# Second layer of a mixture of experts on one core: three token blocks by seven half-width products each, with sums carried between PSUM banks

## The chip, the core and the metric

The kernel runs on one core of a Trainium2 chip. TensorE (PE) multiplies 128x128 tiles; VectorE (DVE), ScalarE (ACT) and GpSimd (POOL) do everything else; DMAs are issued from SyncE (SP). The time is that of the device for one execution, in microseconds (us): the median of three executions unless it is called the profiled one. The changed kernel is timed on the same inputs.

## The reference

Gated linear attention over 4 batches, 8 heads, 768 steps and 48 channels gives x, a 3072 x 384 matrix; router weights P come from its logits by eight Sinkhorn rounds; eight experts then act on every token, each with a hidden layer of 1024.

```python
state = f[:, :, t, :, None] * state + np.einsum('bhd,bhe->bhde', k[:, :, t], v[:, :, t])
y[:, :, t] = np.einsum('bhd,bhde->bhe', q[:, :, t], state)
...
P = np.exp(logits)
for _ in range(8):
    P /= P.sum(1, keepdims=True) + 1e-09
    P /= P.sum(0, keepdims=True) + 1e-09
    P *= N / E
...
for e in range(E):
    h = np.maximum(x @ w1[e], 0.0)
    ye = h @ w2[e]
    out += P[:, e:e + 1] * ye
```

Everything is in float32. The kernel splits each factor of a product into a high and a low fp16 part and sums three matmuls (high with high, low with high, high with low), so one product costs three.

## The kernel before

**Two phases.** Up to about 491 us the attention is computed in chunks, with the plain products of experts 0 and 1 between them; their outputs go unscaled to DRAM, since P isn't known yet, and are fetched, scaled and added later ("re-adds": `yb` by DMA, `yz` by ScalarE, the sum by GpSimd). Phase 2 has 48 periods, for experts 2 to 7, both halves m of the hidden layer and the four batches (`ORDER`). A batch is 768 tokens; a period covers 512 hidden rows of one expert on one batch.

**A period.** The first layer is done by a fast matrix scheme: 15 products on sums of blocks of w1 (`k1`) and of x (`xah`, `xbh`), one per slot (`SLOTS`), each of six matmuls of 256 columns. They accumulate in six PSUM banks named A to F; between them `EVENTS` names what happens after a slot: a copy of a bank to SBUF (ScalarE, `cp`), an add of a copy to a bank (DVE), an init of a fresh bank from another bank and a copy (DVE), and the conversion of a finished bank into the fp16 left factors of the second layer: `kh`/`kl` for a plain half, `kah`/`kal`, and by way of float32 sums `kr`, `kf` the pairs `kgh`/`kgl`. A bank must be complete before the next product adds to it: the init of F reads D, so the third product into D (slot 13) waits for it.

**Second layer before.** Of the three 256-token blocks of a period, t = 0 and 1 are `paired`: the 2 x 2 block product is done with seven half-width products instead of eight (`product`, 42 matmuls of 192 columns), whose partial sums are copied out by ScalarE (`part`), added by GpSimd (L1254, L1255) and DVE (L1257, L1260, L1263) and evicted by DVE (L1216) or by ScalarE and GpSimd (L1219, L1220). Block t = 2 is `plain`: 24 matmuls of 384 columns, evicted by ScalarE and GpSimd. A budget (`drain`) spreads these matmuls over the slots of the next period, from slot `LAG` = 2.

**Weights.** `prepare_w1` and `prepare_w2` run beside it as lists of steps, each at a given slot after its period n (`at_all`, `plan`): a DMA, sums by GpSimd (`k1s`, `k2s`), a maximum over the raw tile for a later check (`wmx`, DVE), high parts by ScalarE and low parts by DVE (`k1l`, L1039; `k2l`, L1053; `k2sl`, L1081). A w1 tile and a w2 tile are prepared in every second period, over some 25 to 39 slots; so an even and an odd period differ, and a pair of them is the unit that repeats.

The order of instructions on every engine is the order in which the program issues them (`pin`, `mm`), whichever is ready. PSUM has eight banks: six rotate for the first layer (`pk`, tag k), two hold second-layer sums (`psm`).

## Time and profile before

| | |
|---|---|
| median of three executions | 1511.97 us (1510.23 to 1512.18) |
| the profiled execution | 1511.74 us, span of its instructions 1510.0 us |
| granted TensorE clock, mean | 0.996 |
| phase 1 | 0 to about 491 us |
| phase 2, 48 periods | about 491 to 1502 us, 20.65 us a period in its steady part |

A row of a timeline has the start, the length, the engine, the line, the operation, what it writes and reads, its shape, and, in brackets, how long the engine had been idle and what ended that. Groups give the total and the mean in ns; a mean includes the latency of one operation, so neighbours overlap by a little. In windows, each engine's busy time stands behind the length of the stretch. A line of waits has the waiting engine and operation, what it waited for, the total, the count and the longest.

### The profile page before, as it was taken

Reading aid. Unit: us, or ns where it says so; the run is one execution under the profiler, and the core shown is the slowest. Engines: PE = TensorE matmul, PEld = TensorE weight load, DVE = VectorE, ACT = ScalarE, POOL = GpSimd, SP = SyncE. Lnnn points to the kernel's source line nnn. Section 1 sums busy time; section 2 is a strip of 40 time slices with the busy share of each in tenths; the row PEclk is TensorE's granted clock in tenths of the full one; section 3 lists DMA queues with packets and bytes.
Section 4 is the critical chain, followed back from the end, with each engine's and each line's share of the span. In section 5 each row is a group of like instructions: output and inputs, shape, how many; then the busy total and the mean of one; then the engine's idle time right before and its main releaser. Section 6 shows DMA issues by size and latency. Waiting matters only on the chain.

```text
span 1510.0 us, 37891 instructions
## 1 busy us (share of the span) xinstructions
PE 1477.1 (98%) x15185; PEld 1213.1 (80%) x15185; DVE 1282.7 (85%) x2352; ACT 1002.8 (66%) x2103; POOL 968.4 (64%) x1154
## 2 busy tenths in 40 slices
...
DMA packets 82794, 95.85 MB, mean 63 GB/s; under 512 B 49872, under 2 KB 66384, under 8 KB 82608
## 3 DMA queue, kind: packets, MB, share of 16 engines
...
## 4 chain that ended last, share of the span: by engine, by line
PE 88%; DVE 7%; ACT 2%; issue 1%; POOL 1%; DMA 1%; DVEq 0%; POOLq 0%; ACTq 0%
PE kyps L287 21%; PE yps L287 13%; PE kxps L287 12%; PE hps L287 10%; PE kb_A L287 8%; PE kb_B L287 8%; PE kb_D L287 6%; PE kb_C L287 4%; PE kb_E L287 2%; PE kb_F L287 2%; PE kvps L287 1%; PE aps L287 1%; DMA w1r<-in_w_dram 1%; DVE kf L1375 1%; POOL k1s L1026 0%
## 5 line engine op out<-in xcount | busy, mean ns | idle before, releaser
L287 PEld LDWEIGHTS <-k1h 128*128 128x128 f16 x2880 | 282.1, 98 | 38.7 <-DVE kl L1392 0.5
L1220 POOL TENSOR_TENSOR acc<-acc,yt 128x384 f32<-128x384 f32 x175 | 203.2, 1168 | 105.7 <-ACT yt L1219 101.2
L1387 POOL TENSOR_TENSOR kgl<-kf,kgh 128x512 f16<-128x512 f32 x188 | 217.1, 1165 | 40.9 <-ACT kgh L1384 40.2
L1219 ACT ACTIVATE yt<-kyps,pes 128x384 f32<-128x384 f32 x175 | 103.7, 592 | 131.8 <-PE kyps L287 69.6
L287 PEld LDWEIGHTS <-kh 128*128 128x128 f16 x1536 | 147.3, 98 | 34.8 <-DVE acc L1212 1.5
L287 PEld LDWEIGHTS <-k1l 128*128 128x128 f16 x1440 | 141.1, 98 | 24.6 <-issue 3.6
L287 PEld LDWEIGHTS <-kgh 128*128 128x128 f16 x1536 | 144.3, 98 | 5.3 <-ACT kgh L1384 1.1
L287 PE MATMUL yps<-w2h,hl 128*128 128x384 f16 x384 | 125.5, 327 | 2.8 <-DVE hl L440 2.6
L287 PE MATMUL yps<-w2l,hh 128*128 128x384 f16 x384 | 125.4, 326 | 1.9 <-DVE w2l L359 1.9
L287 PE MATMUL kyps<-k2h,kh 128*128 128x384 f16 x384 | 125.2, 326 | 1.5 <-DVE acc L1212 1.2
L287 PE MATMUL yps<-w2h,hh 128*128 128x384 f16 x384 | 125.5, 327 | 0.2 <-ACT hh L437 0.2
L287 PE MATMUL kyps<-k2h,kl 128*128 128x384 f16 x384 | 125.2, 326 | 0.4 <-DVE kl L1392 0.4
L287 PE MATMUL kyps<-k2l,kh 128*128 128x384 f16 x384 | 125.2, 326 | 0.0
L287 PEld LDWEIGHTS <-w1h 128*128 128x128 f16 x1344 | 97.2, 98 | 34.0 <-issue 3.1
L1384 ACT ACTIVATE kgh<-kf 128x512 f16<-128x512 f32 x192 | 120.7, 629 | 3.6 <-DVE kf L1375 3.5
L1254 POOL TENSOR_TENSOR part<-part 128x192 f32<-128x192 f32 x96 | 57.3, 596 | 88.7 <-DVE kf L1375 61.1
L287 PEld LDWEIGHTS <-hh 128*128 128x128 f16 x768 | 74.6, 98 | 47.7 <-issue 2.5
L1353 ACT ACTIVATE cp<-kb_A 128x512 f32<-128x512 f32 x144 | 87.4, 607 | 21.9 <-PE kb_A L287 21.6
L287 PE MATMUL kyps<-k2sl,kgh 128*128 128x192 f16 x384 | 94.5, 246 | 0.0
L287 PE MATMUL kyps<-k2sh,kgl 128*128 128x192 f16 x384 | 94.5, 246 | 0.0
L287 PE MATMUL kyps<-k2sh,kgh 128*128 128x192 f16 x384 | 94.5, 246 | 0.0
L287 PEld LDWEIGHTS <-kl 128*128 128x128 f16 x768 | 75.1, 98 | 23.3 <-issue 5.3
...
## 6 DMA issues: line engine op xcount, KB each, us to landing
...
```

The lines of the kernel that those rows point to most:

```text
L287: ins = (nc.tensor.transpose if transpose else nc.tensor.matmul)(**kw)
L1219: pin(nc.scalar.activation(out=yt, in_=ps, func=AF.Copy, scale=p))
L1220: pin(nc.gpsimd.tensor_tensor(out=y, in0=y, in1=yt, op=ALU.add))
L1254: pin(nc.gpsimd.tensor_tensor(out=part[:, 1, :], in0=part[:, 1, :], in1=part[:, 2, :], op=ALU.add))
L1353: pin(nc.scalar.activation(out=fresh(ev[2]), in_=bk, func=AF.Copy))
L1375: pin(nc.vector.scalar_tensor_tensor(out=f[:, n], in0=bk[:, :, 128 * v:128 * v + 128], scalar=0.0, in1=other, op0=ALU.max, op1=op))
L1384: pin(nc.scalar.activation(out=hs['g', t][0][:, lo:hi], in_=hs['f', t][:, lo:hi], func=AF.Copy))
L1387: pin((nc.vector if tag == str(PERIODS - 1) else nc.gpsimd).tensor_tensor(out=hs['g', t][1][:, lo:hi], in0=hs['f', t][:, lo:hi], in1=hs['g ...
```

## The change

All three blocks are `paired`, in another form. A block has one bank, `q`, whose first half is x0, and half of another, `p`, with y0 and x1 (the names are the program's: x0, y0 and x1 are 192 wide each). ScalarE moves sums from bank to bank (`move`, L1179 in the changed kernel: y0 to x0, y0 to x1, x1 to `part`, scaled), and PE goes on accumulating there. DVE adds the finished sums, scaled by P, into the output or into an `yraw` tile (L1182), four 192-wide adds for a block (for block 1 ScalarE does two of them as scaled moves), and GpSimd adds the `yraw` tiles to the output (L1218). Each block takes five slots in a fixed pattern: of its 42 matmuls and its neighbours', slots 8 to 12 of a period have 6, 6, 6, 12 and 12, and so on in fives; the blocks of a period start 6 slots into the next one (`LAG`). In PSUM the first layer has five banks (B and D its own, A, F, E and C rotate over k0 to k2), the second layer one for x and two of `psm`.

The w2 tile keeps three of its four quadrants and four sums, in one tile of 7 x 192 columns, high and low. The steps for a w2 tile are eight for nine: the maximum (step two) moves from slot 12 to slot 22 after the period's start, the lows of the quadrants and the sums to slots 29 and 38. The left factors of the third block add conversions: `gd` and `gb` (differences of two tiles, on GpSimd, for block 2 on DVE), `gs` now in three operations, `kgh`/`kgl` in two pieces for each of three blocks. Copies rotate over two buffers for three, the fetched early output `yb` has one buffer for two, and re-adds begin at period 5 for 3. At the end, 23 slots without first-layer work finish the last blocks.

The diff, cut to what is spoken of:

```diff
-          9: (('ga', 'A', 0),), 10: (('copy', 'C', 7), ('gs', 'A', 0, 0), ('gb', 'A', 0)), 11: (('add', 'D', '-', 7),),
-          12: (('init', 'F', '+', 1, 'D'), ('hh', 'B', 1, 0)), 13: (('gs', 'B', 0, 1), ('gs', 'B', 0, 2), ('gs', 'B', 0, 3)),
-          14: (('gh', 0, 0, 2), ('gl', 0, 0, 2), ('sum', 'D', '-', 4, 3), ('hl', 'B', 1, 0)), 15: (('add', 'C', '+', 3), ('hh', 'D', 1, 2), ('gh', 0, 2, 4), ('gl', 0, 2, 4)),
-          16: (('hh', 'C', 1, 1), ('hh', 'F', 0, 2), ('hl', 'D', 1, 2), ('ga', 'E', 1)), 17: (('hs', 'E', 1), ('hl', 'F', 0, 2)),
-          18: (('gs', 'E', 1, 0), ('gb', 'E', 1)), 19: (('gs', 'C', 1, 1), ('gs', 'C', 1, 2), ('gs', 'C', 1, 3)),
-          20: (('gh', 1, 0, 2), ('gl', 1, 0, 2), ('hl', 'C', 1, 1)), 21: (('gh', 1, 2, 4), ('gl', 1, 2, 4))}
-END = 22
-ENDING = (('add', 'gh', 'gl'), ('ga', 'hs', 'hh'), ('gs',), ('gb', 'hl'), ('gh', 'gl', 'late'))
+          9: (('ga', 'A', 0), ('gd', 0, 'P')), 10: (('copy', 'C', 7), ('gf', 'A', 0)), 11: (('add', 'D', '-', 7), ('hs', 'E', 1)),
+          12: (('init', 'F', '+', 1, 'D'), ('hh', 'B', 0), ('ga', 'E', 1)), 13: (('gs', 'B', 0, 1), ('gs', 'B', 0, 2), ('gs', 'B', 0, 3), ('gb', 1, 'P'), ('gd', 1, 'P')),
+          14: (('gh', 0, 0), ('gl', 0, 0), ('sum', 'D', '-', 4, 3), ('hl', 'B', 0)), 15: (('add', 'C', '+', 3), ('hh', 'D', 2), ('gh', 0, 1), ('gl', 0, 1)),
+          16: (('hs', 'F', 2), ('hh', 'C', 1), ('hl', 'D', 2)), 17: (('ga', 'F', 2), ('gd', 2, 'V'), ('gs', 'D', 2, 1), ('gs', 'D', 2, 2), ('gs', 'D', 2, 3)),
+          18: (('gs', 'C', 1, 1), ('gs', 'C', 1, 2), ('gs', 'C', 1, 3), ('hl', 'C', 1), ('gf', 'F', 2)), 19: (('gh', 1, 0), ('gl', 1, 0)),
+          20: (('gh', 1, 1), ('gl', 1, 1)), 22: (('gh', 2, 0), ('gl', 2, 0)), 23: (('gh', 2, 1), ('gl', 2, 1))}
+END = 24
...
-PLAIN, PAIRED = (2,), (0, 1)
+PAIRED = (0, 1, 2)
+BY_POOL = (1,)
+RIGHTS = ((0, 0), (1, 0), (1, 1))
 DH = DM // 2
-PAIR_COST = 0.51
-PAUSE = 5.0
-LAG = 2
+LAG = 6
 STEPS = 8
+FIRST_READD = 5
...
-    def prepare_w2(e, j, plain_first=False):
+    def prepare_w2(e, j):
...
+        wh, wl = (lp.tile([128, 7, DH], F16, name=f"k2{n}_{e}_{j}", tag=f"k2{n}", bufs=4) for n in "hl")
         (b11, b12), (b21, b22) = ((raw[:, f, 0:DH], raw[:, f, DH:DM]) for f in range(2))
+        pieces = ((wh[:, 0, :], wl[:, 0, :], b11), (wh[:, 1:3, :], wl[:, 1:3, :], raw[:, 1, :].rearrange("p (r d) -> p r d", d=DH)))
+        for h_, _, src in pieces:
+            pin(nc.scalar.activation(out=h_, in_=src, func=AF.Copy, scale=W2S))
+        yield
...
+        lows(pieces)
+        yield
+        pin(nc.scalar.activation(out=wh[:, 3:7, :], in_=sums, func=AF.Copy, scale=W2S))
+        yield
+        lows(((wh[:, 3:7, :], wl[:, 3:7, :], sums),))
+        k2[e, j] = wh, wl
...
-    pk = ctx.enter_context(tc.tile_pool(name="pk", bufs=6, space=PSUM, reuse_waits="tile"))
+    pk = ctx.enter_context(tc.tile_pool(name="pk", bufs=1, space=PSUM, reuse_waits="tile"))
...
+    def paired(n, h, t):
         e, m, b = ORDER[n]
-        if n == first[b]:
+        new = n == first[b]
+        if new and t == PAIRED[0]:
             acc[b] = accp.tile([128, 2, TT, DM], F32, name=f"acc{b}", tag="acc")
-
-        def scale(v, t):
+        p = psm.tile([128, DM], F32, name=f"kyps_{n}_{t}", tag="m")
+        q = pk.tile([128, DM], F32, name=f"kxps_{n}_{t}", tag="x")
+        x0, y0, x1 = q[:, 0:DH], p[:, 0:DH], p[:, DH:DM]
+        p2 = lp.tile([128, DH], F32, name=f"part_{n}_{t}", tag="part", bufs=2)
+        by_pool = t in BY_POOL and n < len(ORDER) - 1 and not new
+        xx, yy = (acc[b][:, v, t, :].rearrange("p (s d) -> p s d", s=2) for v in range(2))
+        if not new:
+            yy = rp.tile([128, 2, DH], F32, name=f"yy_{n}_{t}", tag="yraw", bufs=3)
+        if by_pool:
+            xx = rp.tile([128, 2, DH], F32, name=f"xx_{n}_{t}", tag="yraw", bufs=3)
...
+        def move(out, in_, **kw):
+            pin(nc.scalar.activation(out=out, in_=in_, func=AF.Copy, **kw))
+
+        def add(y, ps, p, z):
+            pin(nc.vector.scalar_tensor_tensor(out=y, in0=ps, scalar=p, in1=z, op0=ALU.mult, op1=ALU.add))
...
+        product(y0, None, (0, 0), start=True)
+        product(x1, (None, 0), (None, 0))
+        yield
+        move(x0, y0)
+        move(p2, x1, scale=scale(1))
+        yield
+        product(y0, (None, 2), (None, 2))
+        yield
+        move(x1, y0)
+        yield
+        product(x0, (1, 0), (1, 0), stop=True)
+        yield
+        yield
+        product(x1, (None, 1), (None, 1))
+        yield
+        out_x(0, x0)
+        add(yy[:, 1, :], x1, scale(1), p2)
+        yield
+        product(y0, (1, 1), (None, 3), stop=True)
+        product(x1, (None, 3), (1, 1), stop=True)
+        yield
+        add(yy[:, 0, :], y0, scale(1), p2)
+        out_x(1, x1)
+        for v, z, there in ((0, xx, not by_pool), (1, yy, new)):
+            if not there:
+                y = acc[b][:, v, t, :]
+                pin((nc.vector if n == len(ORDER) - 1 else nc.gpsimd).tensor_tensor(out=y, in0=y, in1=z.rearrange("p s d -> p (s d)"), op=ALU.add))
...
-            at_all(n, (0, 7, 8, 9, 10, 8, 11, 12, 13, 22, 23, 24) if n else (14, 17, 18, 19, 20, 24, 25, 26, 27, 28, 29, 37), gen)
+            at_all(n, (0, 3, 4, 5, 6, 8, 9, 10, 11, 22, 23, 24) if n else (14, 17, 18, 19, 20, 24, 25, 26, 27, 28, 29, 37), gen)
...
-            at_all(n, (10, 12, 18, 22, 23, 26, 26, 27, 38) if n != 3 else (0, 2, 8, 12, 13, 16, 16, 17, 20), prepare_w2(e2, 2 * m2 + part // 2))
-        if 3 <= n:
-            for s in (9, 12):
-                plan.setdefault((n, s), []).append(lambda: readd(False))
+            at_all(n, (10, 22, 25, 26, 27, 29, 35, 38) if n != 3 else (0, 2, 8, 12, 13, 16, 17, 20), prepare_w2(e2, 2 * m2 + part // 2))
+        if n >= FIRST_READD:
+            at_slots(n, (9, 12), again)
...
+    def kbank(n, bk):
+        k = "AFEC".find(bk)
+        tag = bk if k < 0 else f"k{(max(k - 1, 0) + int(n)) % 3}"
+        return pk.tile([128, 2, 256], F32, name=f"kb_{n}_{bk}", tag=tag)
...
+        elif kind == 'gd':
+            r = hs['r', ev[1]]
+            pin((nc.gpsimd if ev[2] == 'P' else nc.vector).tensor_tensor(out=r[:, 0], in0=r[:, 1], in1=r[:, 0], op=ALU.subtract))
...
+    def advance(n, s):
+        k, j = divmod(n * PRODUCTS + s - LAG, 5)
+        k -= TT
+        if k >= 0 and not j and k < PERIODS * TT:
+            going.append(paired(k // TT, helped[k // TT], PAIRED[k % TT]))
+        if not going or j == 1 and len(going) == 1 and k < PERIODS * TT:
+            return lambda: None
+        block = going[0 if j == 1 else -1]
+        next(block)
+
+        def rest():
+            if next(block, going) is going:
+                going.remove(block)
+
+        return rest
```

Two places on DVE where the order of its instructions moves, both in an odd period (period 11, expert 3; k1l and k2l are the low parts of a w1 and a w2 tile, kb_ the first-layer banks, kxps and kyps second-layer sums, yy and acc output sums). The first is from the second layer's sums at slot 7 to the init of F. Before:

```order
L1216 SCALAR_TENSOR_TENSOR acc_9256<-kxps_0_12046,pes,acc_9256 128x384 [waits DVE_49]
L1263 TENSOR_TENSOR kyps_0_12047<-kyps_0_12047,both_0_12049 128x384 [waits PE_49,Pool_49]
L1355 TENSOR_TENSOR kb_B<-kb_B,cp_0_12141 128x512 [waits Activation_49]
L1039 SCALAR_TENSOR_TENSOR k1l_3_11888<-k1s_3_11802,k1h_3_11887 128x640 x2
L1039 SCALAR_TENSOR_TENSOR k1l_3_11888<-k1r_3_11644,k1h_3_11887 128x256
L1039 SCALAR_TENSOR_TENSOR k1l_3_11888<-k1r_3_11644,k1h_3_11887 128x384
L1375 SCALAR_TENSOR_TENSOR kf_0_12177<-kb_A,kr_0_12180 128x256 [waits PE_49,Activation_49,Pool_49]
L1381 SCALAR_TENSOR_TENSOR kal_0_12197<-kb_A,kah_0_12196 128x256
L1355 TENSOR_TENSOR kb_D<-kb_D,cp_7_12221 128x512 [waits PE_49,Activation_49]
L1053 SCALAR_TENSOR_TENSOR k2l_3_12071<-k2r_3_11873,k2h_3_12070 128x384
L1358 TENSOR_TENSOR kb_F<-kb_D,cp_1_12094 128x512 [waits DVE_49]
```

After:

```order
L1182 SCALAR_TENSOR_TENSOR yy_2_12287<-kyps_2_12284,pes,part_2_12286 128x192 [waits PE_49]
L1182 SCALAR_TENSOR_TENSOR acc_8993<-kyps_2_12284,pes,acc_8993 128x192
L1039 SCALAR_TENSOR_TENSOR k1l_3_12115<-k1s_3_11970,k1h_3_12114 128x640
L1047 TENSOR_REDUCE wmx<-k2r_3_12141 128x1 [waits DMAHW1_49]
L1039 SCALAR_TENSOR_TENSOR k1l_3_12115<-k1s_3_11970,k1h_3_12114 128x640
L1039 SCALAR_TENSOR_TENSOR k1l_3_12115<-k1r_3_11883,k1h_3_12114 128x256
L1039 SCALAR_TENSOR_TENSOR k1l_3_12115<-k1r_3_11883,k1h_3_12114 128x384
L1332 SCALAR_TENSOR_TENSOR kal_0_12483<-kb_A,kah_0_12482 128x256 [waits Activation_49]
L1182 SCALAR_TENSOR_TENSOR acc_9363<-kxps_0_12409,pes,acc_9363 128x192 [waits PE_49]
L1182 SCALAR_TENSOR_TENSOR yy_0_12411<-kyps_0_12408,pes,part_0_12410 128x192 [waits PE_49,Pool_49]
L1302 TENSOR_TENSOR kb_D<-kb_D,cp_7_12505 128x512 [waits Activation_49]
L1305 TENSOR_TENSOR kb_F<-kb_D,cp_1_12367 128x512 [waits DVE_49]
```

The reduction wmx now stands between the k1l operations; the adds of the next block (the two behind kal) come ahead of the add to D; the kf operation and the k2l between D and F have gone from here to behind F.

The second place follows it, from the sum of D and the copy cp_4 to the add that completes A, on which the sixth slot of the next period builds. Before:

```order
L1364 TENSOR_TENSOR cp_3_12308<-kb_D,cp_4_12018 128x512 [waits PE_49]
L1392 SCALAR_TENSOR_TENSOR kl_1_0_11980<-kb_B,kh_1_0_11979 128x512
L1257 TENSOR_TENSOR both_1_12251<-kyps_1_12249,part_1_12250 128x192 [waits Activation_49]
L1355 TENSOR_TENSOR kb_C<-kb_C,cp_3_12308 128x512 [waits DVE_49]
L1392 SCALAR_TENSOR_TENSOR kl_1_2_11984<-kb_D,kh_1_2_11983 128x512 [waits Activation_49]
L1260 TENSOR_TENSOR kxps_1_12248<-kxps_1_12248,both_1_12251 128x192 [waits DVE_49,PE_49]
L1216 SCALAR_TENSOR_TENSOR acc_9256<-kxps_1_12248,pes,acc_9256 128x384 [waits DVE_49]
L1263 TENSOR_TENSOR kyps_1_12249<-kyps_1_12249,both_1_12251 128x384 [waits PE_49,Pool_49]
L1392 SCALAR_TENSOR_TENSOR kl_0_2_11978<-kb_F,kh_0_2_11977 128x512 [waits Activation_49]
L1355 TENSOR_TENSOR kb_A<-kb_A,cp_13_12382 128x512 [waits PE_49,Activation_49]
```

After:

```order
L1064 SCALAR_TENSOR_TENSOR k2l_3_12517<-k2r_3_12141,k2h_3_12516 128x192
L1064 SCALAR_TENSOR_TENSOR k2l_3_12517<-k2r_3_12141,k2h_3_12516 128x384
L1302 TENSOR_TENSOR kb_C<-kb_C,cp_3_12616 128x512 [waits DVE_49]
L1182 SCALAR_TENSOR_TENSOR yy_1_12532<-kyps_1_12529,pes,part_1_12531 128x192 [waits PE_49,Activation_49,Pool_49]
L1351 SCALAR_TENSOR_TENSOR kl_2_12250<-kb_D,kh_2_12249 128x512 [waits Activation_49]
L1326 TENSOR_TENSOR kr_2_12679<-kr_2_12679 128x256 [waits Activation_49]
L1323 SCALAR_TENSOR_TENSOR kr_2_12679<-kb_D,kr_2_12679 128x256 [waits DVE_49]
L1323 SCALAR_TENSOR_TENSOR kf_2_12711<-kb_D,kr_2_12679 128x256
L1323 SCALAR_TENSOR_TENSOR kf_2_12711<-kb_D,kf_2_12711 128x256 [waits DVE_49]
L1182 SCALAR_TENSOR_TENSOR yy_1_12532<-kyps_1_12529,pes,part_1_12531 128x192 [waits PE_49]
L1302 TENSOR_TENSOR kb_A<-kb_A,cp_13_12693 128x512 [waits Activation_49]
```

The two k2l stand here now, with the difference, the sums and a low part for block 2 (kr_2, kf_2, kl_2) and two adds of block 1, where the sums of the paired block and its eviction stood.

273 lines of the change are left out of this document (83 added, 190 removed).

## Prediction, made before the changed kernel had run

> **What bounds the kernel now.** I read the page's engine shares first, then its chain that ended last, then the waits of PE, the windows of one pair of periods, and the timeline of four engines inside that pair. The first two, from the page:
>
> ```profile
> PE 1477.1 (98%) x15185; PEld 1213.1 (80%) x15185; DVE 1282.7 (85%) x2352; ACT 1002.8 (66%) x2103; POOL 968.4 (64%) x1154
> PE 88%; DVE 7%; ACT 2%; issue 1%; POOL 1%; DMA 1%; DVEq 0%; POOLq 0%; ACTq 0%
> ```
>
> PE is busy for 98% of the span and carries 88% of the chain. The shares average two phases, so I look at the steady part of phase 2, where the change lies: two periods (an even and an odd one), by windows, and all of PE's waits between 600 and 1400 us.
>
> ```profile
> 868.50:889.20 20.70, 20.70 (x201) 18.13 (x199) 17.45 (x35) 16.40 (x36) 17.57 (x25) 1.00 0.20 59
> 889.20:909.80 20.60, 20.60 (x200) 18.03 (x199) 20.13 (x37) 15.51 (x33) 16.92 (x19) 1.00 0.19 59
> PE kxps L287 <- DVE acc L1216: 0.5, 1, 0.5
> ```
>
> Columns: length, then PE, PEld, DVE, ACT and POOL busy, then the granted clock. PE has no gap, at clock 1.00; the odd period has DVE at 20.13 of 20.60. So the steady part runs as fast as PE issues matmuls, and DVE is right behind it. That is the whole question: PE gets less to do, DVE does not.
>
> **What PE saves.** Matmuls overlap, so their price is the distance of starts, from PE's timeline:
>
> ```profile
> 900.27 0.33 PE L287 MATMUL kyps<-k2l,kh 128*128 128x384 f16 x1
> ...
> 900.75 0.33 PE L287 MATMUL kyps<-k2l,kh 128*128 128x384 f16 x1
> 900.92 0.25 PE L287 MATMUL kxps<-k2h,kah 128*128 128x192 f16 x1
> ...
> 902.56 0.27 PE L287 MATMUL kb_D<-xah,k1h 128*128 128x256 f16 x1
> ...
> 903.22 0.25 PE L287 MATMUL kyps<-k2sh,kgh 128*128 128x192 f16 x1
> ...
> 904.04 0.27 PE L287 MATMUL kb_F<-xah,k1h 128*128 128x256 f16 x1
> ```
>
> Four 384-wide ones from 900.27 to 900.92 are 0.1625 us each, six 256-wide ones from 902.56 to 903.22 are 0.109, ten 192-wide ones from 903.22 to 904.04 are 0.082. A period has 90 first-layer matmuls, 24 wide and 84 narrow second-layer ones: 9.8 + 3.9 + 6.9 = 20.6 us, which is the window's length. After, the 24 wide ones are gone and 42 narrow ones stand for them: 3.90 - 3.44 = 0.455 us less in each of 48 periods, **-21.9 us**.
>
> Narrower matmuls load weights more often. The loads, by line:
>
> ```profile
> L287 PEld LDWEIGHTS <-k1h 128*128 128x128 f16 x2880 | 282.1, 98 | 38.7 <-DVE kl L1392 0.5
> ```
>
> A load's span is 98 ns, over the 82 ns of a narrow matmul, yet ten narrow ones in a row kept 0.082, so spans of loads overlap and I price them at nothing. The Trainium skill ("TensorE: Matmul & The Clock Gate", section "LDWEIGHTS (loading the stationary operand)") puts a load at its columns over 1.2 in ns, so 107 ns for 128; if that paced PE, 42 narrow matmuls would cost an estimated 4.5 us for the 3.9 of the wide ones, and the change would lose 28 us. The 0.082 us spacing above speaks against that as a pace.
>
> **What DVE, ScalarE and GpSimd get.** ScalarE gives up four evictions and copies of a period and gets about six moves of 192; such a copy is two in 0.55 us here, a move between PSUM banks (512 wide) is 0.58:
>
> ```profile
> 902.76 0.55 ACT L1245 ACTIVATE part<-kxps 128x192 f32<-128x192 f32 x2
> 895.21 0.58 ACT L1361 ACTIVATE kb_C<-kb_B 128x512 f32<-128x512 f32 x1
> ```
>
> With the third block's conversions it goes from some 15.6 to 16.1 us of a period of 20.2: room, price nothing. GpSimd, by groups of the page:
>
> ```profile
> L1220 POOL TENSOR_TENSOR acc<-acc,yt 128x384 f32<-128x384 f32 x175 | 203.2, 1168 | 105.7 <-ACT yt L1219 101.2
> L1387 POOL TENSOR_TENSOR kgl<-kf,kgh 128x512 f16<-128x512 f32 x188 | 217.1, 1165 | 40.9 <-ACT kgh L1384 40.2
> L1254 POOL TENSOR_TENSOR part<-part 128x192 f32<-128x192 f32 x96 | 57.3, 596 | 88.7 <-DVE kf L1375 61.1
> ```
>
> It loses four part adds a period (2.4 us), keeps about four output adds, gets two more kgl (2.3 us) and three 256-wide operations (gd, gd, gb: 0.6 each, worked from the 596 ns of a 192): about +2 us, so 18.5 to 19 us of 20.2 while early outputs are re-added. Its queue then runs late by at most some two slots by my count, and the earliest use of a kgl is about four slots off; no price in the sum, a rival below.
>
> DVE's total falls a little (18.7 to about 18.3 us): eight sums and evictions of two blocks, half of them 384 wide, go and ten 192-wide adds come in. But its order changes, and this is where I find the price. The first place in the section on the change shows what DVE has in odd periods between the x1 product of slot 7 and the init of bank F. F must be made before PE may write D again in slot 13 (the init reads D). Two things are new: the reduction wmx of a w2 tile stands between the four k1l operations (its step moved from slot 12 of the even period to slot 7 of the odd one), and four 192-wide adds stand in the stretch where wider sums came and went earlier. Before, the same stretch, DVE and GpSimd:
>
> ```profile
> 894.49 0.69 DVE L1355 TENSOR_TENSOR kb_B<-kb_B,cp 128x512 f32<-128x512 f32 x1
> 895.09 2.35 DVE L1039 SCALAR_TENSOR_TENSOR k1l<-k1s,k1h 128x640 f16<-128x640 f32 x2
> 897.36 1.68 DVE L1039 SCALAR_TENSOR_TENSOR k1l<-k1r,k1h 128x256 f16<-128x256 f32 x2
> 898.96 0.41 DVE L1375 SCALAR_TENSOR_TENSOR kf<-kb_A,kr 128x256 f32<-128x256 f32 x1
> 899.29 0.41 DVE L1381 SCALAR_TENSOR_TENSOR kal<-kb_A,kah 128x256 f16<-128x256 f32 x1
> 899.62 0.68 DVE L1355 TENSOR_TENSOR kb_D<-kb_D,cp 128x512 f32<-128x512 f32 x1
> 900.22 1.30 DVE L1053 SCALAR_TENSOR_TENSOR k2l<-k2r,k2h 128x384 f16<-128x384 f32 x1
> 901.45 0.69 DVE L1358 TENSOR_TENSOR kb_F<-kb_D,cp 128x512 f32<-128x512 f32 x1
> ```
>
> ```profile
> 895.27 1.48 POOL L1220 TENSOR_TENSOR acc<-acc,yt 128x384 f32<-128x384 f32 x1 [0.17 <-ACT yt L1219]
> 896.72 1.90 POOL L1071 TENSOR_TENSOR k2s<-k2r 128x192 f32<-128x192 f32 x2
> 898.58 1.57 POOL L1074 TENSOR_TENSOR k2s<-k2r,k2s 128x192 f32<-128x192 f32 x2
> 900.11 1.00 POOL L1291 TENSOR_TENSOR acc<-acc,yz 128x384 f32<-128x384 f32 x1
> ```
>
> F ended at 902.14 and PE began D at 902.56: a spare of 0.4 us. The four k1l took 3.87 us (895.09 to 898.96) beside a busy GpSimd. Beside an idle one (idle until 565.39, with 2.78 us of wait before), by the timeline:
>
> ```profile
> 562.60 0.81 DVE L1039 SCALAR_TENSOR_TENSOR k1l<-k1s,k1h 128x640 f16<-128x640 f32 x1
> 563.33 0.95 DVE L1081 SCALAR_TENSOR_TENSOR k2sl<-k2s,k2sh 128x768 f16<-128x768 f32 x1
> 564.20 0.82 DVE L1039 SCALAR_TENSOR_TENSOR k1l<-k1s,k1h 128x640 f16<-128x640 f32 x1
> 564.93 0.89 DVE L1039 SCALAR_TENSOR_TENSOR k1l<-k1r,k1h 128x256 f16<-128x256 f32 x2
> 565.39 1.29 POOL L1291 TENSOR_TENSOR acc<-acc,yz 128x384 f32<-128x384 f32 x1 [2.78 <-ACT yz L1290]
> ```
>
> each 640-wide one is 0.73 from start to start and the last two 0.89: 2.35 in all. The k2l at 900.22 ended at 901.52, half a microsecond after GpSimd's add ended at 901.11, as if it had stood until then. The Trainium skill ("SBUF — State Buffer", section "Who interferes with whom") has VectorE and GpSimd arbitrate for one pair of ports with an exclusive lock; the trace agrees, 3.87 us against 2.35.
>
> Now the chain after, from T, PE's start of slot 8. PE reaches D in slot 13 after 3 slots with 6 narrow matmuls (0.655 + 0.492 = 1.15) and 2 with 12 (1.64): T + 6.7. DVE may start the adds when slot 7's last matmul has landed, T + 0.2. It then does one 192-wide add, wmx, the four k1l, kal, two 192-wide adds, D and F. Prices of the two not yet shown, by groups:
>
> ```profile
> L1260 DVE TENSOR_TENSOR kxps<-kxps,both 128x192 f32<-128x192 f32 x77 | 27.4, 356 | 0.0
> L1049 DVE TENSOR_REDUCE wmx<-k2r 128x1 f32<-128x768 f32 x19 | 17.9, 942 | 0.0
> ```
>
> Neighbours start some 0.08 before the end of one (0.81 against 0.73 above), so 0.3 for an add and 0.86 for wmx; kal 0.33 (899.29 to 899.62 above), D 0.68 since F needs its result, F 0.69. Without contention: 0.2 + 0.3 + 0.86 + 2.35 + 0.33 + 0.6 + 0.68 + 0.69 = 6.0, and PE would not wait. With the four k1l at 3.87: 7.5, and PE waits **0.8 to 0.9**. After, GpSimd is fuller than before in this stretch (kgl and output adds at 1.17), so I take the contended price; its own bound above, where each k1l meets a fresh kgl, is another microsecond. Behind F, DVE has the lows of the w2 tile, the gd, gs, gs, gs of block 2 and the adds before it can finish bank A, on which PE's slot 5 of the next period depends: 7.6 us at lone prices, some 9 contended, with a ScalarE copy (0.6) behind, against 9.0 us of PE. I put 0.45 on it (0 to 1). Even periods have about 1.3 us more room and wait for nothing. Together 1.3 us (0.2 to 2.4) in each of the 20 pairs whose w2 tile is prepared in that place: **+26**.
>
> Head and tail, by windows and waits:
>
> ```profile
> 491.90:507.00 15.10, 13.09 (x109) 10.34 (x107) 11.57 (x20) 10.17 (x20) 5.42 (x7) 1.00 0.12 40
> PE kxps L287 <- ACT part L1245: 1.1, 1, 1.1
> PE kxps L287 <- ACT kgh L1384: 0.9, 1, 0.9
> ```
>
> The first 17 slots, with first-layer work alone, took 15.1 us for 11.1 of matmuls; after, the lag is four slots longer, at 0.23 us lost each: +1. The tail's two waits are on conversions and copies, and there will be a third block's: +1.5 (-1 to +3). The first w2 maximum, which now stands in DVE's row in phase 1, I put inside these.
>
> Sum, from the profiled execution's 1511.74 (span 1510.0, and 0.2 below the median): 1511.7 - 21.9 + 26 + 2.5 = **1518.7 us**.
>
> **Rivals.** *PE stays back to back.* If GpSimd's operations fall beside PSUM-reading adds and wmx, not beside k1l, the 6.0 holds and at most 0.5 us a pair is lost: 1511.7 - 21.9 + 2.5 = 1492.3, up to 1502.3. For it: the uncontended sum has 0.7 us to spare, and before kept PE gapless with DVE at 20.13 of 20.60. Against it: 3.87 is what the k1l cost in the pair shown. It decides below 0.8 us a pair, where the sum passes before's time. Faster; 0.36. *The wait cancels the saving:* 0.8 to 1.1 us a pair, slot 13 alone, 1509 to 1515; 0.14. *The forecast*, 1.1 to 2.2 a pair, 1515 to 1536: 0.39. *GpSimd becomes the bound:* if its operations average their contended spans (1.48 for an add that takes 1.00 elsewhere), it passes 20.2 us in the 24 periods with re-adds, kgl come late and PE waits on weight loads; 1 us in each of 24 on top of the forecast gives 1543. For it: its share is over 90% by count. Against it: the kgl's slack of four slots. 0.08. *Weight loads become the pace:* 198 loads of 98 ns are 19.4 us of before's 20.65; after, 216 are 21.2, over the 20.2 of the matmuls. If loads can't overlap over a whole period as they do over ten, a period is 21.2: 1511.7 + 48 x 0.5 + 2.5 = 1538. Against it: no drift within the ten, and after no narrow run is longer than twelve. 0.03.
>
> **How the numbers follow.** 0.2% (3 us) is about what a measurement can tell from no change. Faster 0.36, same 0.14, slower 0.39 + 0.08 + 0.03 = 0.50. The range leaves out the lower end of the first rival and the last two: 1494 to 1538.
>
> **What would show it.** Right: PE's waits list D or kyps <- DVE F in odd periods some 20 times at about 0.9 us, the span of a pair is about 41.7 us, and PE between waits is 20.2 a period. Wrong: a pair of 40.4 us with no waits of PE on DVE (first rival); PE's weight loads waiting for GpSimd's kgl (third engine); a spacing above 0.083 in long narrow runs (loads); or k1l at 0.73 with GpSimd busy, by which the contended price would be no price.

## The result, and the profile after

The changed kernel takes 1549.42 us (median of four, 1548.40 to 1550.29) against 1512.05: 1.025 times the time before, 95% interval 1.0232 to 1.0268. It is slower, as forecast, but by 37 us where 7 were forecast, and outside the range. Its profiled execution took 1550.04 us, with a span of 1548.3. The page, engine shares and chain:

```profile
PE 1475.1 (95%) x16051; PEld 1264.8 (82%) x16051; DVE 1315.3 (85%) x2510; ACT 1038.4 (67%) x2310; POOL 1066.0 (69%) x1197
PE 54%; DVE 31%; POOL 5%; ACT 5%; issue 4%; DMA 0%; DVEq 0%; POOLq 0%; ACTq 0%
```

PE's part of the chain fell from 88% to 54%, DVE's rose from 7% to 31%: a good part of the bound has moved to DVE. Where in the run the 38.3 us of span came up is read from four points of PE's timeline. Before: the first matmul of phase 2, of its period 1, of its period 47, and PE's last:

```profile
491.90 0.27 PE L287 MATMUL kb_A<-xbh,k1h 128*128 128x256 f16 x1
...
504.07 0.27 PE L287 MATMUL kb_A<-xbh,k1h 128*128 128x256 f16 x1
...
1465.10 0.27 PE L287 MATMUL kb_A<-xbh,k1h 128*128 128x256 f16 x1
...
1501.74 0.33 PE L287 MATMUL kyps<-k2l,kh 128*128 128x384 f16 x1
```

After, the same four, with an odd period (897.22 to 919.60; the periods count from 0, it is number 19), an even one (to 940.30) and the last but one of the run (1475.33 to 1495.55) between them:

```profile
493.39 0.27 PE L287 MATMUL kb_A<-xbh,k1h 128*128 128x256 f16 x1
...
505.62 0.27 PE L287 MATMUL kb_A<-xbh,k1h 128*128 128x256 f16 x1
...
897.22 0.27 PE L287 MATMUL kb_A<-xbh,k1h 128*128 128x256 f16 x1
...
919.60 0.27 PE L287 MATMUL kb_A<-xbh,k1h 128*128 128x256 f16 x1
...
940.30 0.27 PE L287 MATMUL kb_A<-xbh,k1h 128*128 128x256 f16 x1
...
1475.33 0.27 PE L287 MATMUL kb_A<-xbh,k1h 128*128 128x256 f16 x1
...
1495.55 0.27 PE L287 MATMUL kb_A<-xbh,k1h 128*128 128x256 f16 x1
...
1539.94 0.25 PE L287 MATMUL kyps<-k2l,kgh 128*128 128x192 f16 x1
```

Up to period 1: +1.5 us. The 46 periods to 1465.10 and 1495.55: 961.0 before, 989.9 after, +28.9. The end: 36.6 before, 44.4 after, +7.8. Together 38.2.

PE's own saving is there: the period that began at 1475.33, with no weights left to prepare, took 20.22 us where 20.65 was the rule before. But the pair shown took 22.38 + 20.70 = 43.08 for twice 20.22: 2.6 us of waiting, and this is what the prediction had at 1.3. PE in the odd period, and the stretch of DVE and GpSimd that it waits for (slot 7's last products to the init of F):

```profile
898.28 0.25 PE L287 MATMUL kyps<-k2l,kgh 128*128 128x192 f16 x1
898.65 0.28 PE L287 MATMUL kb_B<-xbh,k1h 128*128 128x256 f16 x1
...
904.24 0.25 PE L287 MATMUL kxps<-k2l,kh 128*128 128x192 f16 x1
904.72 0.27 PE L287 MATMUL kb_A<-xbh,k1h 128*128 128x256 f16 x1 [0.23 <-ACT cp L1300]
...
914.86 0.27 PE L287 MATMUL kb_C<-xal,k1h 128*128 128x256 f16 x1
915.96 0.24 PE L287 MATMUL kyps<-k2h,kh 128*128 128x192 f16 x1 [0.83 <-DVE yy L1182]
...
916.87 0.25 PE L287 MATMUL kyps<-k2l,kgh 128*128 128x192 f16 x1
917.30 0.27 PE L287 MATMUL kb_D<-xah,k1h 128*128 128x256 f16 x1 [0.19 <-DVE kb_F L1305]
```

```profile
909.43 0.42 DVE L1182 SCALAR_TENSOR_TENSOR yy<-kyps,pes,part 128x192 f32<-128x192 f32 x1 [0.64 <-PE kyps L287]
909.76 0.41 DVE L1182 SCALAR_TENSOR_TENSOR acc<-kyps,pes,acc 128x192 f32<-128x192 f32 x1
910.08 0.95 DVE L1039 SCALAR_TENSOR_TENSOR k1l<-k1s,k1h 128x640 f16<-128x640 f32 x1
910.96 0.94 DVE L1047 TENSOR_REDUCE wmx<-k2r 128x1 f32<-128x768 f32 x1
911.82 0.81 DVE L1039 SCALAR_TENSOR_TENSOR k1l<-k1s,k1h 128x640 f16<-128x640 f32 x1
912.55 2.38 DVE L1039 SCALAR_TENSOR_TENSOR k1l<-k1r,k1h 128x256 f16<-128x256 f32 x2
914.85 0.41 DVE L1332 SCALAR_TENSOR_TENSOR kal<-kb_A,kah 128x256 f16<-128x256 f32 x1
...
916.55 0.70 DVE L1305 TENSOR_TENSOR kb_F<-kb_D,cp 128x512 f32<-128x512 f32 x1
```

```profile
909.19 1.16 POOL L1346 TENSOR_TENSOR kgl<-kr,kgh 128x512 f16<-128x512 f32 x1 [1.04 <-ACT kgh L1343]
910.31 1.58 POOL L1218 TENSOR_TENSOR acc<-acc,yy 128x384 f32<-128x384 f32 x1
911.86 1.78 POOL L1346 TENSOR_TENSOR kgl<-kf,kgh 128x512 f16<-128x512 f32 x1
913.60 0.91 POOL L1326 TENSOR_TENSOR kr<-kr 128x256 f32<-128x256 f32 x1
```

The start of a matmul less that of the one ahead of it, less its spacing, is PE's gap: 0.99 at 915.96, 0.35 at 917.30, and, early in this period, 0.29 ahead of B at 898.65 and 0.40 ahead of A at 904.72. In the even period behind it the same working gives 0.28 ahead of B (slot 3) and 0.22 ahead of A (slot 5). GpSimd has no pause in these rows; its 512-wide kgl took 1.78 and its add 1.58 where they take 1.16 and 1.0 alone, and DVE's last two k1l together 2.38 where they took 0.89 beside a GpSimd that was idle for half of that time. Both engines pay.

### The profile page after: what moved, and what is told of

It is laid out like the page before. It is cut to its first block, busy times and chain, and to the rows that moved or that the text cites. A ratio compares the mean times of both kernels' runs of the same rounds, so it can differ in the third digit from the quotient of the medians.

```text
span 1548.3 us, 40171 instructions
## 1 busy us (share of the span) xinstructions
PE 1475.1 (95%) x16051; PEld 1264.8 (82%) x16051; DVE 1315.3 (85%) x2510; ACT 1038.4 (67%) x2310; POOL 1066.0 (69%) x1197
## 4 chain that ended last, share of the span: by engine, by line
PE 54%; DVE 31%; POOL 5%; ACT 5%; issue 4%; DMA 0%; DVEq 0%; POOLq 0%; ACTq 0%
PE kyps L287 13%; PE yps L287 13%; PE hps L287 10%; PE kb_A L287 5%; DVE k1l L1039 4%; PE kb_B L287 4%; DVE kf L1323 3%; DVE kl L1351 2%; POOL kgl L1346 2%; DVE yy L1182 2%; DVE k2l L1064 2%; POOL k1s L1026 2%; DVE kr L1326 2%; PE kb_D L287 2%; DVE kr L1323 2%
## 5 line engine op out<-in xcount | busy, mean ns | idle before, releaser
L287 PEld LDWEIGHTS <-k1h 128*128 128x128 f16 x2880 | 282.0, 98 | 40.5 <-DVE kl L1351 11.2
L287 PE MATMUL kyps<-k2h,kgh 128*128 128x192 f16 x1152 | 283.6, 246 | 1.0 <-ACT kyps L1179 1.0
L287 PE MATMUL kyps<-k2l,kgh 128*128 128x192 f16 x1152 | 283.7, 246 | 0.0
L287 PE MATMUL kyps<-k2h,kgl 128*128 128x192 f16 x1152 | 283.7, 246 | 0.0
L287 PEld LDWEIGHTS <-kgh 128*128 128x128 f16 x2304 | 216.8, 98 | 3.2
L1346 POOL TENSOR_TENSOR kgl<-kr,kgh 128x512 f16<-128x512 f32 x141 | 166.5, 1181 | 48.5 <-ACT kgh L1343 48.4
L1182 DVE SCALAR_TENSOR_TENSOR yy<-kyps,pes,part 128x192 f32<-128x192 f32 x264 | 108.3, 410 | 85.3 <-PE kyps L287 82.7
L287 PEld LDWEIGHTS <-k1l 128*128 128x128 f16 x1440 | 141.0, 98 | 38.3 <-issue 28.5
L1218 POOL TENSOR_TENSOR acc<-acc,yy 128x384 f32<-128x384 f32 x129 | 141.4, 1096 | 42.0 <-DVE yy L1182 42.0
L1179 ACT ACTIVATE kxps<-kyps 128x192 f32<-128x192 f32 x144 | 46.6, 324 | 105.4 <-DVE acc L1182 58.7
L287 PEld LDWEIGHTS <-kgl 128*128 128x128 f16 x1152 | 112.8, 98 | 4.6 <-issue 1.2
L1218 POOL TENSOR_TENSOR acc<-acc,xx 128x384 f32<-128x384 f32 x43 | 43.0, 1000 | 74.8 <-ACT xx L1179 74.8
L287 PE MATMUL kyps<-k2h,kh 128*128 128x192 f16 x288 | 70.7, 246 | 22.5 <-DVE yy L1182 21.0
L1343 ACT ACTIVATE kgh<-kr 128x512 f16<-128x512 f32 x144 | 90.7, 630 | 2.0 <-DVE kr L1323 1.9
## 6 DMA issues: line engine op xcount, KB each, us to landing
w1r<-in_w_dram SPq DMA_DIRECT2D x8, 384.0 KB, 10.7
```

The costliest lines, as they stand in the source:

```text
L287: ins = (nc.tensor.transpose if transpose else nc.tensor.matmul)(**kw)
L1179: pin(nc.scalar.activation(out=out, in_=in_, func=AF.Copy, **kw))
L1182: pin(nc.vector.scalar_tensor_tensor(out=y, in0=ps, scalar=p, in1=z, op0=ALU.mult, op1=ALU.add))
L1218: pin((nc.vector if n == len(ORDER) - 1 else nc.gpsimd).tensor_tensor(out=y, in0=y, in1=z.rearrange("p s d -> p (s d)"), op=ALU.add))
L1343: pin(nc.scalar.activation(out=hs['g', t][0][i], in_=hs['f' if i else 'r', t], func=AF.Copy))
L1346: pin((nc.vector if tag == str(PERIODS - 1) else nc.gpsimd).tensor_tensor(out=hs['g', t][1][i], in0=hs['f' if i else 'r', t], in1=hs['g', ...
```

## The experiments

Theory 1 was the prediction's: the chain on DVE sets the wait, and the maximum wmx is its new link. Theory 2: DVE's operations with two SBUF inputs take turns with GpSimd's, and this sets it. Others came up on the way; their numbers are those of the expectations. The stretch is the time on DVE from the start of the first k1l to that of kal, and mean gaps are those of periods 8 to 29 without 21, which has a gap of its own in both kernels. Differences are to 1549.4 (the changed kernel) or, for the kernels made from the one before, to its runs beside them (medians of 1510.6 to 1511.8).

**The maximum (e1, e2).** Moved back in the changed kernel, and moved forward in the kernel before:

```diff
-            at_all(n, (10, 22, 25, 26, 27, 29, 35, 38) if n != 3 else (0, 2, 8, 12, 13, 16, 17, 20), prepare_w2(e2, 2 * m2 + part // 2))
+            at_all(n, (10, 12, 25, 26, 27, 29, 35, 38) if n != 3 else (0, 2, 8, 12, 13, 16, 17, 20), prepare_w2(e2, 2 * m2 + part // 2))
```

In the kernel before (the line of the slots; in `prepare_w2` the step of the high parts now comes ahead of the maximum):

```diff
-            at_all(n, (10, 12, 18, 22, 23, 26, 26, 27, 38) if n != 3 else (0, 2, 8, 12, 13, 16, 16, 17, 20), prepare_w2(e2, 2 * m2 + part // 2))
+            at_all(n, (10, 18, 22, 22, 23, 26, 26, 27, 38) if n != 3 else (0, 2, 8, 12, 13, 16, 16, 17, 20), prepare_w2(e2, 2 * m2 + part // 2))
```

> The changed kernel with the maximum over a w2 tile (wmx) back at slot 12 of the even period instead of slot 22, that is out of the stretch of the four k1l. Theory 1 (the DVE chain between slot 7 and the init of F sets the wait, each operation that leaves it comes off the odd period): the odd period falls from 22.2 us by up to 0.86, some 20 times, 1549 to about 1532; if the maximum is late in its new place, part of that comes back in the even period. Theory 2 (GpSimd's hold on the k1l sets the wait, the maximum only fills time in which they would have stood): no change, 1547 to 1550.

> The kernel before with only this one step of the change: the maximum over a w2 tile at slot 22 instead of slot 12, so that it stands between the k1l of the odd period there too. Theory 1: the spare of 0.4 us ahead of D is used up and 0.86 - 0.4 = 0.46 us a pair is lost, 20 times: 1512 to about 1521, with PE waiting for the init of F in odd periods. Theory 2, or a wait that belongs to the new second layer's sums alone: within 2 us of 1512.

e1: 1553.4, 4 us more, not 17 less. e2: 1510.2, ratio 0.9993 (0.9984 to 1.0003): no loss. The link that theory 1 named falls; DVE's row as such doesn't (d1, below). The stretch in e1's timeline of DVE:

```profile
911.07 2.49 DVE L1039 SCALAR_TENSOR_TENSOR k1l<-k1s,k1h 128x640 f16<-128x640 f32 x2
913.48 2.38 DVE L1039 SCALAR_TENSOR_TENSOR k1l<-k1r,k1h 128x256 f16<-128x256 f32 x2
915.78 0.41 DVE L1332 SCALAR_TENSOR_TENSOR kal<-kb_A,kah 128x256 f16<-128x256 f32 x1
```

4.71 us without the maximum, 4.77 with it (910.08 to 914.85 above); in the kernel before it is 3.87 without and 3.93 with it (e2). It had only filled time in which the second k1l would have stood for GpSimd. The 4 us of e1 come up elsewhere: with the maximum in the even period, PE's gap ahead of B in slot 1 of the odd one is 0.73. By the Trainium skill ("SBUF — State Buffer", section "Who interferes with whom") a reduction never contends for that pair of ports; the trace agrees, 0.94 in both places.

**Two small orders (e3, e4) and a second x area (g2).**

```diff
-          14: (('gh', 0, 0), ('gl', 0, 0), ('sum', 'D', '-', 4, 3), ('hl', 'B', 0)),
+          14: (('gh', 0, 0), ('gl', 0, 0), ('hl', 'B', 0), ('sum', 'D', '-', 4, 3)),
```

```diff
-EVENTS = {1: (('copy', 'A', 4),), 2: (('copy', 'B', 13),),
+EVENTS = {1: (('copy', 'A', 4), ('copy', 'B', 13)),
```

```diff
-        q = pk.tile([128, DM], F32, name=f"kxps_{n}_{t}", tag="x")
+        if not xbank:
+            xbank.append(pk.tile([128, 2, 256], F32, name="kxps", tag="x"))
+        q = xbank[0][:, (n * TT + t) % 2, :]
```

> The changed kernel with the low part of bank B (kl) ahead of the sum of D on DVE, in slot 14. Theory 3 (B has only one bank now, so PE's slot 1 of the next period waits for the kl that reads B): the gap of 0.29 us ahead of B in odd periods goes, 20 x 0.3 = 6 us, 1549 to 1543. Rival: the sum of D and what follows it (the add to C, bank A) are late by the 0.6 us instead, and the time is the same or up to 6 us more.

> The changed kernel with the copy of bank B by ScalarE in slot 1, ahead of the two moves of the second layer's sums, instead of behind them in slot 2. Theory 4 (ScalarE's moves between banks, which wait for PE, hold up the copy for which PE's slot 3 waits): the 0.29 us gap ahead of B in even periods goes, 24 x 0.3 = 7 us, 1549 to 1542, with perhaps some of the 0.2 ahead of A. Rival: the moves are now late and PE waits for those; no change within 2 us.

> The changed kernel with two x areas, the halves of the one x bank in turn, for one. Theory 6 (with one x area ScalarE's move of the next block's sum waits for DVE's add that still reads the area before, 58.7 us in 27 waits, and ScalarE's copies of banks A and B, for which PE waits, stand behind it): those waits go, the gaps of 0.22 and 0.29 us ahead of A and B in even periods and 0.4 ahead of A in odd ones go, some 1 us a pair, 1549 to about 1528. Theory 2 or 5: ScalarE is early but DVE and GpSimd have the same to do; at most 5 us less.

e3: 1557.5, 8 us more, the rival's way and a little past it: the gaps ahead of B in slot 1 and of A in slot 5 of odd periods went, and 0.60 came ahead of A in slot 2 and 0.31 more ahead of B in slot 3. e4: 1549.2, no change: in even periods PE's gap of 0.28 ahead of B went, and the one ahead of A grew from 0.22 to 0.40, with 0.09 ahead of D. g2: 1550.0, no change; ScalarE's wait for the x area is not what holds PE. Three single causes that the waits named, and none carried the time.

**GpSimd's hold (f1, f2, g1).** f1 and f2 replace the four k1l by products of one input with zero (low parts of w1 left out), in either kernel; g1 replaces GpSimd's kgl by fills (low parts of the sums left out).

```diff
-                pin(nc.vector.scalar_tensor_tensor(out=wl[:, at_, :], in0=src, scalar=W1S, in1=wh[:, at_, :], op0=ALU.mult, op1=ALU.subtract))
+                pin(nc.vector.tensor_scalar(out=wl[:, at_, :], in0=src, scalar1=0.0, scalar2=None, op0=ALU.mult))
```

```diff
-            pin((nc.vector if tag == str(PERIODS - 1) else nc.gpsimd).tensor_tensor(out=hs['g', t][1][i], in0=hs['f' if i else 'r', t], in1=hs['g', t][0][i], op=ALU.subtract))
+            pin((nc.vector if tag == str(PERIODS - 1) else nc.gpsimd).memset(hs['g', t][1][i], 0.0))
```

> The changed kernel with the four k1l operations of each w1 tile replaced by a multiplication of one SBUF input by zero (same count, same places, same outputs; the low parts of w1 are left out, so the result lacks them). Theory 2 (DVE's operations with two SBUF inputs wait out GpSimd's; the k1l stretch took 4.77 us with the maximum in it and 4.71 without): the four take some 2.4 us or less beside a busy GpSimd, the waits ahead of slots 12 and 13 in odd periods go, the pair falls from 42.9 towards 41.3, 1549 to about 1522. Theory 5 (DVE's sum of work bounds the pair): the time falls by what DVE is shorter, the same thing here, but without contention the GpSimd operations beside them would not get shorter; they stay at 1.6 to 1.8.

> Control: the kernel before with the same replacement of its k1l (low parts of w1 left out). PE has no gap in its steady part, so shorter k1l are worth nothing there: within 3 us of 1512 by every theory, less a microsecond or two from the head. If it gets faster by over 5 us, the replacement itself does something else.

> The changed kernel with GpSimd's differences kgl (six of 512 columns a period, two SBUF inputs, 1.16 to 1.32 us each) replaced by fills with zeros that read nothing (the low parts of the sums kgh are left out, so the result lacks them). Theory 2 (GpSimd's hold on what DVE's two-input operations need, and its full queue, set the pair): k1l go to about 0.75, gd to 0.55, the pair falls from 42.9 to 41 or less, 1549 to between 1500 and 1515. Theory 5 (DVE's own sum of work is the bound): DVE executes the same operations, so only their stretching by GpSimd goes, some 2 to 3 us a pair at most, 1549 to about 1510 too; but theory 6 (the single x bank couples ScalarE to DVE) expects the even period's 0.5 us of gaps to stay: 20.7.

f1: 1528.9, 20.5 us less; f2, the control: 1509.5, 2 less. g1: 1529.0, 20.4 less. Relief on either side of the pair of engines gives 20 us, and neither gives all of 37; but that the two are equal is chance, for they come from different places. In f1 the stretch is 3.43 for 4.77, and PE's gaps in slots 12 and 13 of odd periods are gone; 0.35 a period comes up in the even ones. In g1 the stretch is longer, 5.26 (4.46 from period 29 on), and so is the gap of the slots 12 and 13 (1.77 for 1.26); what goes is all of the odd period's gaps ahead of B and A (0.75), a part of the even period's, and 3.5 us of the end. So g1 missed what it was made for, the k1l: the 640-wide ones take 1.48 on average, for 0.85 in the changed kernel, and beside them stand GpSimd's other additions. Groups of DVE between 640 and 1080 us, f1 and then g1:

```profile
L1039 DVE TENSOR_SCALAR k1l<-k1r 128x256 f16<-128x256 f32 x11 | 13.7, 1249 | 0.0
L1039 DVE TENSOR_SCALAR k1l<-k1s 128x640 f16<-128x640 f32 x22 | 11.2, 510 | 0.0
```

```profile
L1039 DVE SCALAR_TENSOR_TENSOR k1l<-k1s,k1h 128x640 f16<-128x640 f32 x22 | 32.6, 1482 | 0.0
L1326 DVE TENSOR_TENSOR kr<-kr 128x256 f32<-128x256 f32 x20 | 8.3, 417 | 2.8 <-ACT kr L1315 2.8
```

f1 was not as clean as I meant: a 256-wide one still took 1.25 us, more than a 640-wide one, so it stood although it has one input. The same section of the Trainium skill has such scalar operations as ones that can go into a fast mode with both ports and then contend; these rows agree, with 640 columns in 0.51 us, where the two-input form took 0.81 beside an idle GpSimd, and 256 in 1.25.

In g1 gd (kr) fell to 0.42 us, and here its gain has a cause in the rows. In the changed kernel's odd period gd starts beside a kgl and ends after it, and the add that completes A, its copy and PE's slot 5 (904.72) follow late:

```profile
900.42 1.16 POOL L1346 TENSOR_TENSOR kgl<-kr,kgh 128x512 f16<-128x512 f32 x1
900.46 1.40 DVE L1326 TENSOR_TENSOR kr<-kr 128x256 f32<-128x256 f32 x1 [0.35 <-ACT kr L1315]
903.35 0.69 DVE L1302 TENSOR_TENSOR kb_A<-kb_A,cp 128x512 f32<-128x512 f32 x1
904.07 0.60 ACT L1300 ACTIVATE cp<-kb_A 128x512 f32<-128x512 f32 x1
```

With gd at 0.42 the gap ahead of A in odd periods is gone; it is gone in e1 too, where gd takes 0.73 there.

**Load moved between the two (f3, f4).**

```diff
-          16: (('hs', 'F', 2), ('hh', 'C', 1), ('hl', 'D', 2)), 17: (('ga', 'F', 2), ('gd', 2, 'V'),
+          16: (('hs', 'F', 2), ('hh', 'C', 1), ('hl', 'D', 2)), 17: (('ga', 'F', 2), ('gd', 2, 'P'),
```

```diff
-BY_POOL = (1,)
+BY_POOL = ()
```

> The changed kernel with the difference gd of block 2 on GpSimd instead of DVE (there it has two SBUF inputs and takes 0.55 alone, 1.40 us beside a busy GpSimd). Theory 5 (DVE's sum of work is the bound): 0.5 to 1 us a period less, 1549 to between 1505 and 1525. Theory 2 (the two engines share one resource): the difference takes 0.8 us of GpSimd instead; the time stays within 10 us of 1549, either side.

> The changed kernel with block 1's x sums added by DVE straight from PSUM (two 192-wide adds of 0.33 us more a period) instead of moved by ScalarE and added by GpSimd (one addition of 1.0 us less). Theory 5 (DVE's sum of work is the bound): 0.65 us more in each of 47 periods, 1549 to about 1575 to 1580. Theory 2 (GpSimd's hold is the bound): no change or up to 10 us less, since an operation that reads PSUM does not stand behind GpSimd.

f3: 1589.9, 40.5 us more, far past every expectation: PE now waits for DVE's kf, which waits for gd behind GpSimd's row. f4: 1558.9, 9.5 more, less than the 26 to 31 that DVE's sum of work asked for, and not the gain or the nothing of theory 2 either. Of these two moves, the one onto GpSimd, which I had priced at nothing, was the worse.

**Order and number (g3, g4, d1, d2, d3, d4).** g3 puts the first k1l at slot 13 of the even period:

```diff
-            at_all(n, (0, 3, 4, 5, 6, 8, 9, 10, 11, 22, 23, 24) if n else (14, 17, 18, 19, 20, 24, 25, 26, 27, 28, 29, 37), gen)
+            at_all(n, (0, 3, 4, 5, 6, 8, 9, 10, 11, 13, 22, 24) if n else (14, 17, 18, 19, 20, 24, 25, 26, 27, 28, 29, 37), gen)
```

g4 runs a slot's weight preparation ahead of the second layer's adds:

```diff
-            rest()
             for job in plan.pop((n, s), []):
                 job()
+            rest()
```

d1 makes the two 640-wide k1l one of 1280 columns; d2 does that and makes the other two one of 768 (with `WPOS` and the tile's width to match); d3 is d2 with g4; d4 is d1's edit in the kernel before:

```diff
-        for parts in (halves[:1], halves[1:], ones):
+        for parts in (((slice(0, 10), sums[:, 0:10]),), (), ones):
             for at_, src in parts:
                 pin(nc.vector.scalar_tensor_tensor(
```

```diff
-        ones = ((slice(10, 12), raw[:, 0:2, 0:128]), (slice(12, 15), raw[:, 0:3, 128:256]))
+        ones = ((slice(10, 16), raw.rearrange("p a (h d) -> p (a h) d", h=2)),)
```

> The changed kernel with the first k1l at slot 13 of the even period instead of slot 7 of the odd one, and the others a slot later or where they were. Theory 2 and 5 in one form (the odd period's DVE row is too long, the even one has room): about 0.9 us of the odd period's row moves to the even one, the pair falls by 0.5 to 0.9, 1549 to between 1530 and 1538. If the two k1l left stand as long as three (as happened when the maximum left that stretch): no change.

> The changed kernel with a slot's weight preparation ahead of the second layer's adds on every engine, instead of behind them. Theory 7 (DVE stands 0.64 us in slot 7 for PE's x1 product, 82.7 us in 73 such waits over the run, with the k1l behind the add that waits): the k1l fills that wait, up to 0.6 us a pair comes off, 1549 to about 1537. Theory 2: the k1l waits for GpSimd just as long wherever it stands; no change, or later adds and up to 5 us more.

> The changed kernel with the two 640-wide k1l of a w1 tile as one of 1280 columns: the same elements, three operations for four. Theory 8 (each two-input operation of DVE stands until one GpSimd operation has ended, whatever its own length, so the number counts): one turn of some 0.8 to 1.2 us less in the odd period, up to 20 of them come off, 1549 to about 1530 to 1537. Theory 5 (DVE's sum of work): the same work, no change within 3 us.

> The changed kernel with the four k1l of a w1 tile as two, of 1280 and 768 columns (the last takes 128 columns along that nothing reads, 0.13 us more). Theory 8: two turns less, 1549 to about 1520 to 1530. Theory 5: 0.13 us more a pair, no change within 3 us.

> The changed kernel with the k1l as two operations and with a slot's weight preparation ahead of the second layer's adds (which alone took 10.7 us off). Theory 8 with 7: the two causes are different waits and add up in part, 1549 to about 1512 to 1522. If both stood for the same GpSimd operations, no better than the better one alone, 1525 to 1538. It would beat the kernel before only if nearly all waits in the steady part went, since head and tail alone are some 9 us longer.

> Control: the kernel before with one 1280-wide k1l for two of 640. PE has no gap in its steady part, so a shorter DVE row is worth nothing there by every theory: within 3 us of 1511.

g3: 1551.9, 2.5 more: the gaps of slots 12 and 13 go, but the moved k1l makes the low part kl of B late, and the gap ahead of B in slot 1 grows from 0.29 to 1.64. g4: 1538.8, 10.7 less. d1: 1538.1, 11.4 less, with the same elements to work on. d2: 1539.2, no further gain. d3: 1529.1, ratio 1.0116 (1.0099 to 1.0133), 20.3 less: the two gains in sum, though both act on the gaps of slots 12 and 13. d4, the control: 1511.1, no change. d1's stretch on DVE:

```profile
906.12 1.61 DVE L1039 SCALAR_TENSOR_TENSOR k1l<-k1s,k1h 128x1280 f16<-128x1280 f32 x1
907.65 0.94 DVE L1047 TENSOR_REDUCE wmx<-k2r 128x1 f32<-128x768 f32 x1
908.52 1.84 DVE L1039 SCALAR_TENSOR_TENSOR k1l<-k1r,k1h 128x256 f16<-128x256 f32 x2
910.28 0.41 DVE L1332 SCALAR_TENSOR_TENSOR kal<-kb_A,kah 128x256 f16<-128x256 f32 x1
```

906.12 to 910.28 is 4.16 us for 4.77. PE's gap in slot 12 fell by as much, from 0.91 to 0.31 on average, and no other gap changed by more than 0.02; 20 times 0.6 is about the gain. This shows that DVE's row up to F sets PE's gaps in slots 12 and 13, and that the number of operations that meet GpSimd counts beside their work. d2 takes the stretch to 3.26 and those gaps to nothing, and yet gains no more: the odd period falls from 22.26 to 21.00, but the even one rises from 20.71 to 21.63, with PE waiting in slots 2 to 5 for what DVE does behind F. That d2's time stood still says nothing against theory 8; a second link had come up behind the first. d3 is the best form found of the change, and still slower than the kernel before.

**Adds one slot later (h2, and h1 on top of d3).** The last two adds of a block, kept in a list and run in the next slot:

```diff
+            while ended:
+                next(ended.pop(0), None)
+            if j == 1 and k < PERIODS * TT:
+                going.remove(block)
+                ended.append(block)
-            if next(block, going) is going:
+            elif next(block, going) is going:
                 going.remove(block)
```

> The changed kernel with k1l in two operations, weight preparation ahead of the adds, and the last two adds of each block one slot later, so that DVE finds PE's product done. Theory 7: DVE's waits for PE (33 us in 31 waits between 640 and 1080 us with the other two changes) mostly go; what PE still waits for DVE falls with them, 1529 to about 1515 to 1522, and in the best case the kernel before (1512) is reached. If the remaining gaps are ScalarE's copies and GpSimd's results: no change from 1529.

> The changed kernel with only the last two adds of each block one slot later. Theory 7: as much as by the weight preparation ahead of the adds, 1549 to about 1535 to 1540, by the same mechanism in another way. Theory 2 alone: the k1l stand for GpSimd wherever they are; no change within 4 us.

h1: 1634.9, h2: 1646.6, near 100 us more than without it. ScalarE in h2, and PE behind it:

```profile
907.57 0.39 ACT L1329 ACTIVATE kah<-kb_F 128x256 f16<-128x256 f32 x1
911.94 0.42 ACT L1179 ACTIVATE xx<-kyps,pes 128x192 f32<-128x192 f32 x1 [3.97 <-DVE yy L1182]
912.25 0.32 ACT L1179 ACTIVATE kyps<-kyps 128x192 f32<-128x192 f32 x1
912.50 0.59 ACT L1300 ACTIVATE cp<-kb_A 128x512 f32<-128x512 f32 x1
```

```profile
910.07 0.25 PE L287 MATMUL kxps<-k2l,kh 128*128 128x192 f16 x1
913.14 0.37 PE L287 MATMUL kb_A<-xbh,k1h 128*128 128x256 f16 x1 [2.83 <-ACT cp L1300]
```

I had looked at DVE's row alone. Block 1's x sums are moved by ScalarE, in the same step; ScalarE's move waits behind DVE's add, which now stands at the end of a full row, and the copy of A for which PE waits stands behind the move. Not all of the 97 us is waiting: by the spacing of the matmuls' starts in the two traces I estimate some 70 us of added gaps and some 29 us of matmuls at about half speed behind such gaps (the last section shows one). In the changed kernel too moves stand ahead of the copies of A and B, but e4 and g2, which relieve them, gain nothing.

## Why the prediction was wrong

The forecast was 31 us short: some 23 in the waits of the steady part, 7 at head and tail, the rest in small differences.

**Direction, PE's saving and the loads: right.** 0.43 us a period against 0.455. The twelve narrow matmuls from 915.96 to 916.87 are 0.083 apart, no drift, and a whole period without waits took 20.22 us, where loads as the pace would have made 21.2; the rival of the weight loads is out.

**DVE's row up to F in the odd period: right in place, 0.5 short in size.** F was forecast to end at T + 7.5 with T = 909.22, PE's slot 8; it ended at 917.25, T + 8.0. PE lost 0.99 + 0.35 = 1.34 there against 0.8 to 0.9, most of it one slot earlier than named: in slot 12 PE waits for DVE's add yy, which stands ahead of F in the same row. Of the miss, 0.33 is plain: two adds stand ahead of the k1l, as the rows in the section on the change show, and I counted one. The stretch itself came out as added (0.86 + 3.87 = 4.73 against 4.77), but by luck: the maximum adds 0.06 and not 0.86 (e1, e2), and the k1l alone take 4.71 where 3.87 was their price. Why they are longer than before stays open. GpSimd has kgl of 512 columns there now, where the sums k2s of 192 stood; but with the kgl gone (g1) the stretch was longer while the re-adds ran (5.26) and hardly shorter after them (4.46 for 4.63). Shown is that the stretch sets PE's gap (d1).

**Bank A behind F: right.** The 0.45 was for DVE's row behind F, up to the add into A for slot 5 of the next, even, period. That period took 20.70, 0.5 over 20.22: 0.28 ahead of B and 0.22 ahead of A. With B's copy early (e4) the wait went over to A, so the add into A is the later end; this is argued from e4's gaps. From period 30 on it is 0.25 ahead of D and 0.40 ahead of A.

**"Even periods have room and wait for nothing": wrong, and the largest miss of the steady part.** The even period's row on DVE ends in the odd period, in its first slots. There PE lost 0.75 in the pair shown, for which the sum had nothing: 0.29 ahead of B in slot 1 (B has one bank of its own now, and PE's weight load ahead of it waits for the kl that reads it), 0.06 in slot 3, and 0.40 ahead of A in slot 5, late by gd, which took 1.40 beside a kgl and 0.42 without (g1). With the kgl replaced, all of the 0.75 went.

**ScalarE "room, price nothing":** what was tried bears it out for the changed kernel (e4, g2). But its share of 67% is no proof of that: its row is in order, and h2 shows what one late move does to the copies behind it.

**Steady part in sum:** 1.34 + 0.50 + 0.75 is 2.59 of the 2.64 us of the pair; forecast 0.85 + 0.45. Over the 46 periods the waits are 59.8 us (989.9 less 46 times 20.22) against 11.1 before, 48.7 more, where 26 was forecast.

**GpSimd as the bound, put at 0.08:** the sign that was given for it, PE's weight loads waiting for kgl, didn't show; of other engines, they list DVE's kl alone between 640 and 1080 us. It doesn't bound by its share. But by meeting DVE's operations it lengthens DVE's row and is lengthened by it, and the sum had that for the odd period's row alone.

**Head and tail: +2.5 forecast, +9.3 measured.** Phase 2 begins 1.5 us later. In phase 1 the two traces of PE run level from 40 us to 72 us and 1.0 apart from there on: the hoisted maximum stood in DVE's row at 71.45 us, after 0.4 us of waiting for its DMA, and PE waited 0.82 us for the low part hl behind it. Another 0.4 is from five first touches of the PSUM banks (`kb_touch`) for three. The end is 7.8 us longer. By the larger `LAG` 407 matmuls are left from the start of period 47 on, for 319 before; by their spacings that is 36.5 us for 32.9, so 3.6 of the 7.8 is work that came later. The rest is waits: without first-layer work between them, the last blocks show each link of the new form (ScalarE's move, DVE's add, the next product) as a wait of PE, the two longest 1.9 and 2.0 us for DVE's adds. This is counted from the traces; no run took it apart.
